# Column halves for the last rows, a masked table for the first unit, and a second queue for the tail stores

**Chip and metric.** One core of a Trainium2 chip. The time is device microseconds (us) of one execution. Runs of a kernel on one chip spread by up to 5 us.

## The reference

Sliding-window attention over q, k, v of shape (8, 8, 576, 64) makes x (8 batches, 576 tokens, 512 channels). Then comes a mix in the frequency domain:

```python
X = np.fft.rfft(x, axis=1)
Y[:, :64] = X[:, :64] times a complex 512 x 512 matrix per mode   # w_r, w_i: 134 MB read
y = np.fft.irfft(Y, n=S, axis=1)
u = x + y
out = u + np.maximum(u @ w_ch, 0.0)                                # 9.44 MB written
```

## The kernel before

For most of its time the kernel reads the 64 modes' weights. While they come, it collects the spectral rows Z (Y as rows of modes) and ZW (Y times w_ch) of the modes that are done. When the last weight has landed, the last mode's rows have to be scaled, transposed, multiplied by w_ch and patched into Z and ZW with small DMAs. Then 18 output units (128 tokens of two batches each; units 8 and 17 are the "tail" units of 64-token remainders) are made and stored.

The passage from the last weight to the first unit:

```python
yq, yT = heads[LAST]
nc.scalar.mul(yq[96:], acc[96:], 2.0 / S)
scatter([nc.sync, nc.scalar, nc.sync, nc.sync, nc.scalar, nc.gpsimd, nc.gpsimd, nc.gpsimd],
        yq, LAST, 6, 8, lambda b: Z[:, b])           # 8 small DMAs, two of them from ScalarE
... # 4 transposes into tr
nc.vector.tensor_copy(yT[:, :, 96:], tr[:, :, 96:])
... # heads["yw"] = late_channels(...): 4 matmuls with w_ch, then nc.scalar.copy(yw, zl)
take(1); begin(1); channels(1)
patch_channels([nc.sync] + [nc.gpsimd] * (B - 1), heads["yw"], LAST)
for step in ("a0 f0 a1 f1 a2 a3 f3 a5 f5 a10 f2 a8 f8 a12 f10 a9 f9 a11 f12 a14 f14 "
             "a16 f11 a17 f17 a4 f16 a6 f6 a7 a13 f4 f13 a15 f15 f7").split(): ...
```

A unit is made by `activate` (aN: matmuls into mm, relu by ScalarE into r; for the units in POOLED GpSimd adds the tokens to r) and `finish` (fN: matmuls into yy, for the others with the tokens added on TensorE; VectorE adds yy and r into o; o is stored). The first two units take the last rows of ZW not from the patched ZW but through a masked table FM, so they need not wait for the patches.

```python
POOLED, HALVES, FIRST = (2, 4, 7, 10, 11, 12, 16), (0, 1, 3, 5, 7), (0, 1)
...
for half in range(2):                                 # tail units: 64 partitions per store
    lo, hi = b + half + 2 * c.start, b + half + 2 * c.stop - 1
    nc.sync.dma_start(out=out[lo:hi:2, FULL * P :].rearrange("b p e -> p b e"),
                      in_=o[ROWS[half], c])
```

The softmax here doesn't subtract the row's maximum and nothing guards it: scores larger than these inputs give would overflow.

## Time and profile before

| | before |
|---|---|
| time, median of 3 runs (4 with the one beside the changed kernel's) | 450.82 us (450.8) |
| span of the profiled run | 449.1 us |
| last weight landed | 411.04 us |
| its last matmul ends | 412.26 us |
| first store issued | 417.79 us |
| last matmul ends | 440.5 us |
| last data of the stores | 447.5 us |

In a line of the chain of waits the columns are start, length and what held the end up. In a stretch of the window view come, after the stretch and its length, busy us (and instructions) of TensorE, its weight loads, VectorE, ScalarE and GpSimd, then TensorE's clock, the busy share of the 16 DMA engines, and GB/s. The prediction shows these lines for the kernel before.

### The profile page before, as it was taken

Reading aid. Unit: us, or ns where it says so; the run is one execution under the profiler, and the core shown is the slowest. Engines: PE = TensorE matmul, PEld = TensorE weight load, DVE = VectorE, ACT = ScalarE, POOL = GpSimd, SP = SyncE. Lnnn points to the kernel's source line nnn. Section 1 sums busy time; section 2 is a strip of 40 time slices with the busy share of each in tenths; the row PEclk is TensorE's granted clock in tenths of the full one; section 3 lists DMA queues with packets and bytes.
Section 4 is the critical chain, followed back from the end, with each engine's and each line's share of the span. In section 5 each row is a group of like instructions: output and inputs, shape, how many; then the busy total and the mean of one; then the engine's idle time right before and its main releaser. Section 6 shows DMA issues by size and latency. Waiting matters only on the chain.

```text
span 449.1 us, 7986 instructions
## 1 busy us (share of the span) xinstructions
PE 350.6 (78%) x3291; PEld 188.1 (42%) x3315; DVE 176.9 (39%) x321; ACT 152.2 (34%) x193; POOL 72.8 (16%) x124
## 2 busy tenths in 40 slices
PE   4688899999866485467477768999999998866992
PEld 3456777777654132122122334444444443322330
DVE  7879899998832011000010223121221203301783
ACT  6869899999810000000000011112211110100771
POOL 8600101012411100100000000000000000074771
PEclk8689999999999568875965799999999999999998
DMA  8999999999999999999999999999999999994698
GB/s 281 311 314 322 302 311 313 316 306 241 207 292 316 306 286 316 326 379 424 420 420 422 422 422 419 419 422 417 422 419 419 422 420 421 420 392 146 239 304 307
DMA packets 53607, 157.03 MB, mean 350 GB/s; under 512 B 5172, under 2 KB 24388, under 8 KB 41156
## 3 DMA queue, kind: packets, MB, share of 16 engines
q1 hardware_dynamic: 47708, 140.54, 81.4%
q0 software_dynamic: 5856, 15.99, 18.1%
q8 instruction: 26, 0.43, 0.4%
q14 instruction: 9, 0.07, 0.0%
q10 hardware_dynamic: 8, 0.00, 0.0%
HBM read 162.53 MB, written 9.44 MB: 383 GB/s over the span
## 4 chain that ended last, share of the span: by engine, by line
DMA 60%; PE 27%; DVE 8%; issue 2%; SPq 1%; POOL 0%; ACT 0%; DVEq 0%; POOLq 0%
DMA w<-in_moe_w_i_dram 19%; DMA w<-in_moe_w_r_dram 16%; DMA vr<-in_v_dram 15%; PE acc L822 10%; DMA vr<-in_moe_w_i_dram 7%; PE my L671 7%; DVE vb L233 3%; PE tr L650 2%; PE my L628 2%; DMA kr<-in_k_dram 2%; DMA out_dram<-o 1%; PE yy L762 1%; PE mm L704 1%; PE yy L748 1%; DVE vt L235 1%
## 5 line engine op out<-in xcount | busy, mean ns | idle before, releaser
L822 PE MATMUL acc<-w,XC 128*32 128x512 bf16 x456 | 127.9, 449 | 45.5 <-DMA w<-in_moe_w_r_dram 26.8
L822 PEld LDWEIGHTS <-XC 128*32 128x32 bf16 x508 | 59.4, 140 | 126.3 <-issue 89.5
L294 ACT ACTIVATE att<-sc 128x1024 bf16<-128x1024 f32 x64 | 64.1, 1032 | 7.7 <-PE sc L284 7.7
L605 ACT CAST ZW<-zw 128x512 bf16<-128x512 f32 x8 | 4.7, 585 | 161.4 <-DVE Z L607 126.3
L577 DVE TENSOR_SCALAR yq<-acc 128x512 bf16<-128x512 f32 x13 | 8.9, 688 | 100.2 <-PE acc L822 100.2
L680 ACT CAST XW<-my 128x512 bf16<-128x512 f32 x36 | 19.3, 589 | 75.4 <-PE my L628 75.4
L618 POOL DMA_DIRECT2D Z<-yq x19 | 9.7, 517 | 213.5 <-issue 207.9
L331 PE MATMUL av<-vb,att 128*128 128x132 bf16 (+1 forms) x576 | 38.4, 217 | 5.8 <-DVE x L347 4.1
L331 PEld LDWEIGHTS <-att 128*128 128x128 bf16 x704 | 36.5, 98 | 11.4 <-DVE x L347 8.4
L652 DVE COPY xT<-tr 128x1024 bf16<-128x1024 bf16 x18 | 12.5, 692 | 69.7 <-PE tr L650 69.7
L671 PE MATMUL my<-wch,xT 128*64 128x512 bf16 x288 | 34.5, 382 | 0.8 <-DVE xT L652 0.8
L256 ACT COPY qkT<-tp 128x1152 bf16<-128x1152 bf16 x30 | 33.4, 1115 | 3.0 <-PE tp L250 2.4
L284 PE MATMUL sc<-qkT 64*64 64x256 bf16 (+2 forms) x640 | 25.4, 266 | 5.2 <-ACT qkT L256 1.6
L347 DVE TENSOR_TENSOR x<-av,rec 128x640 bf16<-128x640 f32 x32 | 26.4, 825 | 1.1
L774 DVE TENSOR_TENSOR o<-yy,r 128x1024 f32<-128x1024 f32 (+1 forms) x23 | 21.7, 988 | 7.6 <-ACT r L739 5.9
L671 PEld LDWEIGHTS <-xT 128*64 128x64 bf16 x288 | 14.8, 109 | 18.9 <-issue 6.9
L284 PEld LDWEIGHTS <-qkT 64*64 64x64 bf16 x640 | 14.6, 109 | 19.1 <-issue 15.8
L233 DVE CAST vb<-vr 64x1024 bf16<-64x1024 f32 x32 | 22.2, 694 | 0.2
L607 DVE CAST Z<-z 64x512 bf16<-64x512 f32 x16 | 11.0, 689 | 24.6 <-PE z L600 24.4
L305 DVE TENSOR_TENSOR att<-att,mask 128x1024 bf16<-128x1024 bf16 x32 | 20.6, 683 | 0.0
L739 ACT ACTIVATE r<-mm 128x1024 f32<-128x1024 f32 (+1 forms) x23 | 18.4, 839 | 5.8 <-PE mm L628 4.9
L523 POOL COPY gate<-x 1x1 bf16<-1x1 bf16 x11 | 5.8, 525 | 85.8 <-DVE x L347 85.8
(119 smaller groups left out, 372.6 us busy)
## 6 DMA issues: line engine op xcount, KB each, us to landing
w<-in_moe_w_i_dram SPq DMA_DIRECT2D x52, 1024.0 KB, 18.0
w<-in_moe_w_r_dram SPq DMA_DIRECT2D x45, 1024.0 KB, 17.9
qr<-in_q_dram SPq DMA_DIRECT2D x16, 576.0 KB, 9.6
kr<-in_k_dram SPq DMA_DIRECT2D x16, 576.0 KB, 6.3
vr<-in_v_dram SPq DMA_DIRECT2D x64, 128.0 KB, 6.1
w<-in_moe_w_r_dram POOLq DMA_DIRECT2D x16, 512.0 KB, 17.2
out_dram<-o SPq DMA_DIRECT2D x11, 512.0 KB, 3.6
out_dram<-o SPq DMA_DIRECT2D x14, 256.0 KB, 3.7
```

The lines of the kernel that those rows point to most:

```text
L233: nc.vector.tensor_copy(self.vb[u % 2][row, :, :, :, W * half : W * half + D], src[row, :2])
L256: (self.nc.vector.tensor_copy if u < 2 and w == "q" else self.nc.scalar.copy)(dst.rearrange("q h (p j) -> q h p j", j=TPP), tp.rearrange(" ...
L284: nc.tensor.matmul(sc[64 * half : 64 * half + 64, e, j * 256 + c0 : j * 256 + c0 + n], lhsT=qkT[row, 1, h, k0 + j : k0 + P : 2], rhs=qkT[r ...
L294: self.nc.scalar.activation(self.att[u % 2][:, kt * 8 * P : (kt + 1) * 8 * P], sc.rearrange("p e n -> p (e n)"), AF.Exp, scale=1.0 / math. ...
L305: nc.vector.tensor_tensor(out=rows, in0=rows, in1=self.table[:, heads], op=ALU.mult)
L331: nc.tensor.matmul(bank[:, qt * W : qt * W + rhs[j].shape[1]], lhsT=att[:, o : o + P], rhs=rhs[j], start=(n == 0 and j == 0), stop=(n == l ...
L347: nc.vector.tensor_tensor(out=self.x[:, b, :, cs].rearrange("p t (h d) -> p h t d", h=2), in0=tiles[:, :, :, :D], in1=rec.unsqueeze(-1).br ...
L671: nc.tensor.matmul(mm[ROWS[half]], lhsT=lhsT, rhs=wch[:, dt], start=(dt == 0), stop=False, skip_group_check=True,)
L680: nc.scalar.copy(XW[:, j, n], mms[n])
L739: nc.scalar.activation(r[:, c], mm[:, c], AF.Relu)
L774: nc.vector.tensor_tensor(out=o[:, c], in0=yy[:, c], in1=r[:, c], op=ALU.add)
L822: nc.tensor.matmul(into[32 * (i // 2) : 32 * (i // 2) + 32], lhsT=window[a], rhs=w[a], start=(ri == 0 and a == 0), stop=(ri == (m > 0) and ...
```

## The change

The intent is to shorten the passage and to keep the stores fed and fast. The last rows go through ScalarE, transposes and w_ch in two halves of 256 columns, and ScalarE issues no DMA any more. Unit 0 takes its Y rows through FM as well (its other Y matmuls move in front of the last weight). The second half of each tail store goes to GpSimd's queue. The order of units, and which units GpSimd adds to, change too. One more thing is in the diff: a matmul into zl whose result is overwritten (L889, issued at 412.55, 0.39 us) stands before the transposes.

```diff
-        POOLED, HALVES, FIRST = (2, 4, 7, 10, 11, 12, 16), (0, 1, 3, 5, 7), (0, 1)
+        POOLED, HALVES, FIRST = (3, 4, 8, 12, 16), (0, 1, 2, 7, 15), (0, 1)
 ...
+            if j == 0:
+                last_rows(yys[0][0], 0, heads["yq"])
 ...
-                    nc.sync.dma_start(
+                    (nc.gpsimd if half else nc.sync).dma_start(
                         out=out[lo:hi:2, FULL * P :].rearrange("b p e -> p b e"),
 ...
                     add_tokens(0)
+                    finish_tokens(0)                 # in front of the last weight's matmuls
 ...
-        nc.scalar.mul(yq[96:], acc[96:], 2.0 / S)
-        scatter([nc.sync, nc.scalar, nc.sync, nc.sync, nc.scalar, nc.gpsimd, ...
+        for i, c in enumerate(sides):                # two halves of 256 columns
+            nc.scalar.mul(yq[96:, c], acc[96:, c], 2.0 / S)
+            ... # 2 transposes
+            nc.vector.tensor_copy(yT[:, 2 * i : 2 * i + 2, 96:], tr[:, 2 * i : 2 * i + 2, 96:])
+        patch([(nc.sync, 0), (nc.sync, 1)], yq, LAST, lambda b: Z[:, b])
+        patch([(nc.gpsimd, b) for b in (2, 3, 4)], yq, LAST, lambda b: Z[:, b], 6)
+        yw = F[:, : DM // (2 * NM)].rearrange("p a b -> p (a b)")   # a dead table as buffer
+        for i, c in enumerate(sides):
+            late_channels(zl[i], yT, yw, c)
 ...
+        channel_rows([(nc.sync, 0)] + [(nc.gpsimd, b) for b in (1, 2, 3)])
+        patch([(nc.gpsimd, b) for b in (5, 6, 7)], yq, LAST, lambda b: Z[:, b], 6)
+        channel_rows([(nc.gpsimd, b) for b in (4, 5, 6, 7)])
-        ... "a0 f0 a1 f1 a2 a3 f3 a5 f5 a10 f2 a8 f8 a12 f10 a9 f9 a11 f12 a14 f14 "
-            "a16 f11 a17 f17 a4 f16 a6 f6 a7 a13 f4 f13 a15 f15 f7"
+        ... "a0 f0 a1 f1 a3 a2 f2 a7 f7 a4 f3 a5 f5 a16 a9 f4 f9 a12 a17 f16 f17 a8 "
+            "a13 f12 f13 a11 f11 a14 f8 a10 f14 a6 f10 f6 a15 f15"
```

More of the change, by code (lines that the diff above doesn't have):

```diff
@@ L547, in late_end @@
             nc.vector.tensor_scalar_mul(yq[rows], acc[rows], 2.0 / S)
-            scatter([nc.gpsimd] * B, yq, g, 0, 2 * n, lambda b: Z[:, b])
+            patch([(nc.gpsimd, b) for b in range(2 if g == LAST else 0, B)],
+                  yq, g, lambda b: Z[:, b], 0, 2 * n)
             yield
@@ L560, in late_end, with late_channels @@
             zw = ps.tile([P, DM], FP32, tag="zw", bufs=1, name="zw")
-            patch_channels([nc.gpsimd] * B, late_channels(zw, yT), g)
-        def late_channels(zw, yT):
+            yw = pool.tile([P, DM], BF16, tag="yq", bufs=3)
+            late_channels(zw, yT, yw, slice(0, DM))
+            patch([(nc.gpsimd, b) for b in range(B)], yw, g, lambda b: ZW[:, b // 2, 1])
+        def late_channels(zw, yT, yw, c):
             for et in range(4):
-                nc.tensor.matmul(zw, lhsT=yT[:, et], rhs=wch[:, et],
+                nc.tensor.matmul(zw[:, c], lhsT=yT[:, et], rhs=wch[:, et, c],
                                  start=(et == 0), stop=(et == 3))
-            yw = pool.tile([P, DM], BF16, tag="yq", bufs=3)
-            nc.scalar.copy(yw, zw)
-            return yw
-        def patch_channels(queues, yw, g):
-            scatter(queues, yw, g, 0, 8, lambda b: ZW[:, b // 2, 1])
+            nc.scalar.copy(yw[:, c], zw[:, c])
         def quad_end(acc, g):
@@ L612, in stream_spectra, with patch @@
             spectra(hf, bp, z, zw)
-        def scatter(queues, rows, g, lo, hi, dst):
-            for b in range(B):
+        def patch(todo, rows, g, dst, lo=0, hi=8):
+            for queue, b in todo:
                 r = 64 * (b % 2) + 8 * (g % 8)
-                queues[b].dma_start(out=dst(b)[r + lo : r + hi],
-                                    in_=rows.rearrange("(k v) e -> k v e", v=16)[lo:hi, b])
+                queue.dma_start(out=dst(b)[r + lo : r + hi],
+                                in_=rows.rearrange("(k v) e -> k v e", v=16)[lo:hi, b])
         def tokens(st, half):
@@ L717, in channels, with last_rows @@
                         spread(mm[:, n], row, b + row + 2 * n, 1, st, 0)
-        def last_channels(j):
-            mm, st = mms[j][0], units[j][1]
+        def last_rows(ps, j, rows):
+            st = units[j][1]
             for n in range(2):
-                nc.tensor.matmul(mm[:, n], lhsT=FM[:, n, st * P : (st + 1) * P], rhs=heads["yw"],
+                nc.tensor.matmul(ps[:, n], lhsT=FM[:, n, st * P : (st + 1) * P], rhs=rows,
                                  start=False, stop=True, skip_group_check=True)
@@ L731, in activate @@
             if j in FIRST:
-                last_channels(j)
+                last_rows(mms[j][0], j, heads["yw"])
             else:
@@ L749, in add_tokens, with finish_tokens @@
                                  start=True, stop=False, skip_group_check=True)
-        def finish(j):
-            b, st = units[j]
-            if j not in yys:
-                take(j)
-            if j and j not in POOLED:
-                add_tokens(j)
-            (yy, slot), r = yys.pop(j), rs.pop(j)
-            o = heads["out"].tile([P, 2, DM], FP32, tag="o", bufs=5, name="o")
+        def finish_tokens(j):
+            yy, b, st = yys[j][0], *units[j]
             for n in range(2):
@@ L772, in finish @@
                     )
+        def finish(j):
+            b, st = units[j]
+            if j == 0:
+                last_rows(yys[0][0], 0, heads["yq"])
+            else:
+                if j not in yys:
+                    take(j)
+                if j not in POOLED:
+                    add_tokens(j)
+                finish_tokens(j)
+            (yy, slot), r = yys.pop(j), rs.pop(j)
+            o = heads["out"].tile([P, 2, DM], FP32, tag="o", bufs=5, name="o")
             for c in parts(j):
@@ L878 @@
         yq, yT = heads[LAST]
-        nc.scalar.mul(yq[96:], acc[96:], 2.0 / S)
-        scatter([nc.sync, nc.scalar, nc.sync, nc.sync, nc.scalar, nc.gpsimd, nc.gpsimd, nc.gpsimd],
-                yq, LAST, 6, 8, lambda b: Z[:, b])
-        tr = lps.tile([P, 4, P], BF16, tag="tr", name="tr")
-        for et in range(4):
-            nc.tensor.transpose(tr[:, et, 96:], yq[96:, et * P : (et + 1) * P], ident[96:, 96:])
-        nc.vector.tensor_copy(yT[:, :, 96:], tr[:, :, 96:])
-        with ExitStack() as zctx:
-            zps = zctx.enter_context(tc.tile_pool(name="zps", bufs=1, space=PSUM))
-            heads["yw"] = late_channels(zps.tile([P, DM], FP32, name="zl"), yT)
+        zctx = ExitStack()
+        zps = zctx.enter_context(tc.tile_pool(name="zps", bufs=1, space=PSUM))
+        zl = [zps.tile([P, DM], FP32, name=f"zl{i}") for i in range(2)]
+        nc.tensor.matmul(zl[1], lhsT=ident, rhs=wch[:, 0], start=True, stop=True)
+        sides = (slice(0, DM // 2), slice(DM // 2, DM))
+        tr = lps.tile([P, 4, P], BF16, tag="tr", name="tr")
+        for i, c in enumerate(sides):
+            nc.scalar.mul(yq[96:, c], acc[96:, c], 2.0 / S)
+            for et in (2 * i, 2 * i + 1):
+                nc.tensor.transpose(tr[:, et, 96:], yq[96:, et * P : (et + 1) * P],
+                                    ident[96:, 96:])
+            nc.vector.tensor_copy(yT[:, 2 * i : 2 * i + 2, 96:], tr[:, 2 * i : 2 * i + 2, 96:])
[4 more added lines that the diff above has]
+            late_channels(zl[i], yT, yw, c)
+        zctx.close()
         lctx.close()
@@ L891 @@
             tc.tile_pool(name="tps", bufs=1, side="right", space=PSUM, reuse_waits="tile"))
+        heads.update(yq=yq, yw=yw)
         heads["mm"].append(last)
@@ L898 @@
         channels(1)
-        patch_channels([nc.sync] + [nc.gpsimd] * (B - 1), heads["yw"], LAST)
-        for step in ("a0 f0 a1 f1 a2 a3 f3 a5 f5 a10 f2 a8 f8 a12 f10 a9 f9 a11 f12 a14 f14 "
-                     "a16 f11 a17 f17 a4 f16 a6 f6 a7 a13 f4 f13 a15 f15 f7").split():
+        channel_rows = partial(patch, rows=yw, g=LAST, dst=lambda b: ZW[:, b // 2, 1])
+        channel_rows([(nc.sync, 0)] + [(nc.gpsimd, b) for b in (1, 2, 3)])
+        patch([(nc.gpsimd, b) for b in (5, 6, 7)], yq, LAST, lambda b: Z[:, b], 6)
+        channel_rows([(nc.gpsimd, b) for b in (4, 5, 6, 7)])
+        for step in ("a0 f0 a1 f1 a3 a2 f2 a7 f7 a4 f3 a5 f5 a16 a9 f4 f9 a12 a17 f16 f17 a8 "
+                     "a13 f12 f13 a11 f11 a14 f8 a10 f14 a6 f10 f6 a15 f15").split():
             {"a": activate, "f": finish}[step[0]](int(step[1:]))
```

## The prediction

> **What bounds the kernel now.** I read the page first, then the chain of waits from 380 us on, then the timeline from 405 us on, and last the engines and the DMA in stretches of that tail. Up to about 409 us the weight stream sets the pace (its DMA lines hold 19%, 16% and 7% of the page's chain), and the change leaves that part as it is. All that matters lies in the last 40 us.
>
> The chain of waits (start us, us, what):
>
> ```profile
> 408.77 1.07 PE acc L822 x4
> ...
> 411.14 1.14 PE acc L822 x4
> 412.27 0.02 issue
> 412.29 0.60 ACT yq L879
> 412.89 0.28 issue
> 413.17 0.49 POOL Z L618
> 413.66 1.51 DMA Z<-yq
> 415.18 0.59 ACT yw L568
> 415.76 0.04 issue
> 415.81 0.59 PE mm L723 x2
> ...
> 434.60 0.61 SPq L784
> 435.21 0.05 issue
> 435.26 4.85 DMA out_dram<-o
> ```
>
> The last weight is multiplied until 412.27. Then a serial passage of 3.54 us leads to the first matmul that makes an output (415.81). From there the chain is TensorE without a break until 433.27, and after that the stores. So the tail has three stages: the passage, a stage at TensorE's pace, and a drain of the stores.
>
> The timeline of the passage:
>
> ```profile
> 412.91 1.85 ACTq L618 DMA_DIRECT2D Z<-yq  x2
> 413.52 1.04 PE L565 MATMUL zl<-wch,xT 128*128 128x512 bf16 x4 [0.32 <-DVE xT L885]
> 415.17 0.58 ACT L568 CAST yw<-zl 128x512 bf16<-128x512 f32 x1 [2.29 <-DMA Z<-yq]
> 417.79 6.83 SPq L776 DMA_DIRECT2D out_dram<-o  x9
> ```
>
> zl is complete at 414.56, but ScalarE copies it only at 415.17: its own two DMA issues last until 414.76, and the profile names a Z DMA as what the copy waited for (its buffer comes from the pool that those DMAs read). That is 0.6 us of avoidable wait. The first store is issued at 417.79, 5.52 us after the last weight.
>
> Stretches of the store stage (the last two numbers of a line are DMA share and GB/s):
>
> ```profile
> 418.00:426.00 8.00, 7.85 (x70) 2.43 (x74) 6.32 (x9) 6.19 (x10) 6.03 (x6) 1.00 0.85 306
> 426.00:427.00 1.00, 0.95 (x10) 0.32 (x8) 1.00 (x2) 0.93 (x2) 0.45 (x1) 1.00 0.58 219
> 427.00:429.00 2.00, 2.00 (x20) 0.40 (x18) 1.70 (x3) 1.50 (x2) 1.68 (x1) 1.00 0.72 143
> 429.00:436.00 7.00, 6.85 (x57) 2.05 (x58) 5.69 (x5) 5.21 (x6) 5.30 (x3) 1.00 1.03 367
> 436.00:439.00 3.00, 3.00 (x31) 0.99 (x24) 2.74 (x3) 2.08 (x4) 2.40 (x2) 1.00 0.94 274
> 439.00:447.00 8.00, 1.43 (x6) 0.39 (x4) 3.36 (x4) 0.94 (x1) 0.83 (x1) 0.85 1.03 383
> ```
>
> The page counts 9.44 MB written. At 383 GB/s that is 24.6 us, yet the data move from about 418.6 to 447.5, that is 28.9 us: 4.3 us of store time are lost. Each stretch loses length x (383 - rate) / 383: 1.6 us in the first (part of it before any store), 0.4 in 426 to 427, 1.25 in 427 to 429, 0.3, and 0.85 in 436 to 439. The 1.25 and the 0.85 follow the two pairs of tail-token stores (issued from 426.19 and 434.60). One microsecond shows how:
>
> ```profile
> 428.00:429.00 1.00, 1.00 (x14) 0.20 (x10) 1.00 (x2) 0.93 (x1) 0.68 (x1) 1.00 0.98 182
> ...
> 433.00:434.00 1.00, 1.00 (x13) 0.26 (x10) 0.65 (x1) 0.37 (x2) 0.92 (x1) 1.00 1.04 391
> ```
>
> At 428 the DMA engines are as busy as at 433 and move less than half. This is slow data, not missing data.
>
> **What the Trainium skill says.** (1) "SBUF — State Buffer", section "Door 1: The DMA port swizzle": partitions 0 to 63 reach only 8 of the 16 ports, 64 to 127 the other 8. A tail store reads 64 partitions; 182 against 391 GB/s agrees. (2) Same page, "Can I just issue two DMAs to hit both halves?": it answers no, with 6% gained. That speaks against one part of the change; nothing in the trace before tests it. (3) "DMA: Bandwidth & Descriptors", "Queues, rings and completion order": each DMA engine takes turns, packet by packet, between the queues that have work. So a half on a second queue at least interleaves with the other half or with the next full store. Not tested before either. (4) "TensorE: Matmul & The Clock Gate", "Back-to-back issue gap": a 512-column matmul every 216 ns, 256 columns about 109. The chain's pairs of 0.43 us (0.215 each) agree.
>
> **The change part by part.** (a) Unit 0's two Y matmuls move in front of the last weight. The last weight DMA is issued at 391.5 and lands after 19.6 us, at 411.1; the matmuls for it start at 411.14, directly behind other work of TensorE, so the two extra ones delay them: 2 x 0.215 = +0.43 us on the path. Their counterparts with the masked table take, after the passage, the place of the two removed: no change there.
>
> (b) The passage. Before, from 412.27 to 415.81: 0.62 scaling, 0.35 to the copy of the transposes, 0.28 to zl, 1.04 zl, 0.61 wait, 0.64 copy and start. After: two scalings of 256 columns end together about where one of 512 did (0.64); transposes and copy of the second half about 0.45 (before 0.58, for half the size); zl in two halves, 4 x 0.107 + 0.19 until ScalarE may copy the first, 0.43 later the second; that last copy is half as long (0.33); no DMA issues on ScalarE and a dead table as the buffer, so no wait. Sum: 0.64 + 0.45 + 0.62 + 0.43 + 0.33 + 0.08 = 2.55. But unit 1's begin and channel matmuls (0.64) stand behind zl on TensorE and end near 2.6, so I take 2.65: -0.89 us. With (a) the first store comes 0.46 us earlier, near 417.33.
>
> (c) Units added on GpSimd go from 7 to 5. Each unit that goes back to TensorE adds two identity matmuls, by the timeline 1.52 us between begins against 1.10, so 2 x 0.42, less the tail unit that goes the other way (same 0.5 in another place): TensorE's sum over units 2 to 17 goes from 22.5 to 23.3 us, and TensorE ends at 440.9 instead of 440.5. GpSimd has 13 patch issues (about 0.53 each) after the passage instead of 10, so its first addition can start near 420.8 instead of 419.84. The new order places that unit's finish third, where VectorE wants it at about 422.9: just in time.
>
> (d) The tail halves go to two queues. If they then use both port groups, the loss of 1.25 + 0.85 us shrinks to the gaps for missing data; I count 1.2 us of 2.1 regained.
>
> (e) The order of units. Dealing out 1.2 us per VectorE output and 1.37 us per full store (524 KB at 383 GB/s) from 417.3 on, stores wait for data about 1.5 us in all before 426 and hardly after. Before, the first two stretches lose 2.0 us, and part of 427 to 429 is missing data too (share 0.45 in its first half, by the same view). I count 0.8 us regained.
>
> Sum: -0.46 - 1.2 - 0.8 = -2.5 us; 450.82 - 2.5 = 448.3. Cross-check: TensorE ends at 440.9, VectorE needs two halves of 0.62 to 0.68 after it, issue and start about 0.9, data 0.7, and from the last data (447.5) to the end of the span 1.6 pass: 445.6 at the very least, 3.5 under 449.1. So time can hardly go below 447, since TensorE is the next bound.
>
> **The rivals.** Rival 1: the two queues do not help (the skill's 6%). Then the tail stores still need 2 x 64-partition time, gains are (b), (e) and little else: about 449.5. For it: the page's statement. Against it: the packets of the second queue can interleave with a full store. Rival 2: TensorE's or GpSimd's extra work becomes the bound. 13 patches hold GpSimd longer; a patch that lands late (one took 3.5 us once stores ran, 419.24 to 422.73) can stop TensorE at unit 16, which needs the last batches early. One such stop costs 0.5 to 1.5 us: 449 to 450. Rival 3: all is hidden, because the stores at the end are limited by bytes alone. Against it: 4.3 us of 28.9 are lost, so bytes alone do not set the end. It would give 450.4 (only the earlier start counts). Rival 4: more works out than I count (all 2.1 us of the tails and no stalls): 447.0.
>
> **Range and chances.** Predicted 448.3 us; 8 times in 10 between 446.8 and 450.0: the low end is TensorE's bound with some error in (c), the high end is rival 1 or 2 with noise (the three runs before differ by 1 us). A change of 2% is 9 us, more than twice all lost store time, so faster by over 2% has 1%; slower by over 2% would take 9 us of stalls, which nothing in the trace suggests: 1%. Within 2%: 98%.
>
> **What would show it.** Right: last weight's matmuls ending near 412.7; ScalarE's copies in halves with no wait for a DMA; first store near 417.3; full rate (over 330 GB/s) in the microseconds after the tail stores; TensorE's last matmul near 441 and last data near 445. Wrong: the last weight not delayed (then (a) is mis-sized); a stretch with share near 1.0 and about 180 GB/s after the tail stores (rival 1); TensorE or VectorE idle for GpSimd or a patch DMA (rival 2). A different landing time of the last weight would shift everything.

## The result and the profile after

The changed kernel takes 452.56 us (451.44 to 453.07, 4 runs) against 450.8 us before: slower by 0.32%, with a 95% interval of 0.10% to 0.55%. A ratio here is the mean time of one kernel's runs over that of the other's of the same rounds, so it is not quite the ratio of the medians. I had predicted 448.3 with a range up to 450.0: wrong.

The passage did what it should. The chain of waits of the changed kernel, its passage and its end:

```profile
411.57 1.06 PE acc L829 x4
412.63 0.02 issue
412.65 0.39 ACT yq L893
413.04 0.05 issue
413.08 0.22 PE tr L895 x2
...
413.77 1.11 PE zl L568 x8
414.89 0.34 PE mm L702 x4
415.23 0.22 PE mm L626 x4
415.45 0.54 PE mm L721 x2
...
441.20 0.69 DVE o L780
```

From 412.63 to 415.45 it lasts 2.82 us (3.54 before), and no ScalarE wait for a DMA is in it. VectorE's last output, too, ends at 441.89, no later than before. What is lost comes after that, in the drain. The timeline of the changed kernel at the first tail pair and at GpSimd's first additions:

```profile
417.37 13.30 SPq L782 DMA_DIRECT2D out_dram<-o  x13
...
421.38 4.23 POOL L740 TENSOR_TENSOR r<-r,x 128x1024 f32<-128x1024 f32 x2
...
423.56 4.75 DVE L780 TENSOR_TENSOR o<-yy,r 128x1024 f32<-128x1024 f32 x4 [0.90 <-POOL r L740]
...
431.43 0.73 SPq L790 DMA_DIRECT2D out_dram<-o  x1
...
431.70 0.66 POOL L790 DMA_DIRECT2D out_dram<-o  x1 [0.86 <-DVE o L780]
```

The first store is issued at 417.37, 0.42 us earlier than before. GpSimd's first addition starts at 421.38, and VectorE waits 0.90 us for it. Stretches of one microsecond of the changed kernel, at the first tail pair and at the end:

```profile
433.00:434.00 1.00, 1.00 (x12) 0.31 (x4) 1.00 (x2) 0.64 (x1) 1.00 (x1) 1.00 1.00 184
434.00:435.00 1.00, 1.00 (x12) 0.28 (x12) 0.92 (x2) 0.50 (x2) 0.52 (x1) 1.00 1.08 285
435.00:436.00 1.00, 1.00 (x13) 0.26 (x10) 1.00 (x2) 0.92 (x2) 0.00 (x0) 1.00 0.88 272
...
446.00:447.00 1.00, 0.00 (x0) 0.00 (x0) 0.00 (x0) 0.00 (x0) 0.00 (x0) 0.50 0.88 336
447.00:448.00 1.00, 0.00 (x0) 0.00 (x0) 0.00 (x0) 0.00 (x0) 0.00 (x0) 0.50 0.35 135
448.00:449.00 1.00, 0.00 (x0) 0.00 (x0) 0.00 (x0) 0.00 (x0) 0.00 (x0) 0.50 0.08 29
```

The same end of the kernel before:

```profile
446.00:447.00 1.00, 0.00 (x0) 0.00 (x0) 0.00 (x0) 0.00 (x0) 0.00 (x0) 0.50 1.04 391
447.00:448.00 1.00, 0.00 (x0) 0.00 (x0) 0.00 (x0) 0.00 (x0) 0.00 (x0) 0.50 0.27 100
```

Two things are to be seen. The first half of the tail pair still runs at about half rate (184 GB/s at share 1.00), and by the packet records it runs alone: GpSimd's half, issued at 431.70, has its first packet at 434.20, 2.5 us later. And before, all DMA engines work until about 447.2 and stop together, while in the changed kernel the share falls from 0.88 over 0.35 to 0.08: a few engines work on alone for over a microsecond. By the packet records what they still move are SyncE's stores, not GpSimd's, at 84 ns a packet, as in the full stores before: these engines are not slow at the end, they have more left to do. The last data come at 448.7 instead of 447.5, although the last store is issued only 0.3 us later (444.18 against 443.85).

### The profile page after: what moved, and what is told of

It reads as the page before. It is cut to its first block, busy times and chain, and to the rows that moved or that the text cites. A ratio compares the mean times of both kernels' runs of the same rounds, so it can differ in the third digit from the quotient of the medians.

```text
span 450.1 us, 8002 instructions
## 1 busy us (share of the span) xinstructions
PE 355.8 (79%) x3301; PEld 191.5 (43%) x3326; DVE 176.9 (39%) x322; ACT 152.7 (34%) x195; POOL 70.5 (16%) x125
## 4 chain that ended last, share of the span: by engine, by line
DMA 47%; PE 34%; DVE 12%; issue 2%; ACT 1%; POOL 1%; SPq 0%; DVEq 0%; POOLq 0%; ACTq 0%
DMA w<-in_moe_w_r_dram 25%; PE acc L829 10%; DMA w<-in_moe_w_i_dram 10%; PE my L669 7%; DMA vr<-in_moe_w_r_dram 7%; DMA vr<-in_v_dram 5%; DVE vb L233 3%; PE tr L648 2%; PE my L626 2%; PE av L331 2%; DVE x L347 2%; PE yy L754 1%; PE mm L702 1%; DVE att L305 1%; PE yy L746 1%
## 5 line engine op out<-in xcount | busy, mean ns | idle before, releaser
L829 PE MATMUL acc<-w,XC 128*32 128x512 bf16 x456 | 129.4, 450 | 45.3 <-DMA w<-in_moe_w_r_dram 25.8
L284 PE MATMUL sc<-qkT 64*64 64x256 bf16 (+2 forms) x640 | 25.7, 269 | 4.8 <-ACT qkT L256 1.2
```

Of the source, the lines that this page charges most:

```text
L284: nc.tensor.matmul(sc[64 * half : 64 * half + 64, e, j * 256 + c0 : j * 256 + c0 + n], lhsT=qkT[row, 1, h, k0 + j : k0 + P : 2], rhs=qkT[r ...
L829: nc.tensor.matmul(into[32 * (i // 2) : 32 * (i // 2) + 32], lhsT=window[a], rhs=w[a], start=(ri == 0 and a == 0), stop=(ri == (m > 0) and ...
```

## The experiments

**How they are compared.** Up to the last weight's landing the kernels do the same, but that landing fell anywhere between 410.5 and 413.9 us in the profiled runs, and this noise is larger than the differences sought. So beside the time ratio I use the stretch from the last weight's landing (from the DMA completions in the trace) to the end of the span. Two control runs say how well it repeats: unaltered copies of both kernels gave 38.04 us (38.06 at first) and 39.06 us (39.05). "Engines full until" is when 14 or more packets were last in flight, counted in the trace's packet records (good to about 0.2 us). A stretch is called dry when the DMA engines have too few stores to move, and a trickle when only a few of them still move data. All times but the ratio are us after the landing.

| kernel | time against before (95%) | first store | engines full until | last data | end |
|---|---|---|---|---|---|
| before; again | 0.998 (0.995 to 1.001) | 6.74; 6.62 | 36.2; 36.1 | 36.46; 36.45 | 38.06; 38.04 |
| changed; again | 1.0032; 1.0031 (1.000 to 1.006) | 6.30; 6.12 | 35.5; 36.0 | 37.61; 37.63 | 39.05; 39.06 |
| e1 tail on one queue | 0.9977 (0.995 to 1.0005) | 6.30 | 35.9 | 36.19 | 37.51 |
| e2 before + two queues | 0.9994 (0.997 to 1.002) | 6.63 | 35.8 | 36.94 | 38.19 |
| e3 passage only | 1.0044 (1.002 to 1.007) | 6.39 | 38.1 | 38.38 | 39.69 |
| e4 order only | 0.9987 (0.996 to 1.001) | 6.71 | 35.6 | 36.36 | 37.97 |
| e5 tail: SyncE and ScalarE | 1.0011 (0.997 to 1.005) | 6.09 | 35.4 | 36.74 | 38.04 |
| e6 unit 5 before 3 | 1.0011 (0.998 to 1.004) | 6.29 | 35.6 | 36.58 | 37.89 |
| e8 tail: both GpSimd | 1.0028 (0.999 to 1.007) | 6.34 | 36.3 | 38.46 | 40.01 |
| e9 tail early | 1.0008 (0.997 to 1.0045) | 6.33 | 35.7 | 36.94 | 38.25 |
| e10 tail early, two queues | 1.0001 (0.997 to 1.003) | 6.18 | 35.6 | 37.21 | 38.62 |
| e12 unit 3 on TensorE | 0.9977 (0.995 to 1.0005) | 6.39 | 35.4 | 36.42 | 37.72 |
| e13 full store on GpSimd | 0.9967 (0.994 to 0.999) | 6.28 | 35.3 | 37.48 | 38.83 |

**The changed kernel and the kernel before, again.** No edit.

> The changed kernel once more, unaltered, as a control beside the other runs: 0.3% above before, and from the landing of the last weight to the end of the span 39.0 us again (the kernel before has 38.06), with DMA engines finishing at different times. If that stretch comes out under 38.5, one profile is not enough to compare tails by.

> The kernel before, unaltered, as a control of the method: ratio 1.000 within 0.2%, and from the landing of the last weight to the end of the span 38.06 us again, within 0.2 us. If the stretch differs by more than 0.5 us, differences of tails of that size mean nothing.

Measured: stretches of 39.06 and 38.04 us, ratios 1.0031 and 0.998. So the stretch repeats to 0.02 us for these two, and the change costs 1.0 us of it. Of the other 0.4 of the 1.4 us (0.31% of 452), 0.25 us is outside the span: in the changed kernel's runs the time exceeds the span by 2.2 us on average, in those of before by 1.97. I have no explanation for these 0.25 us; e3, without a GpSimd store, shows 2.3. What is left, 0.15 us, is well within the interval.

**e1, the tail stores on one queue**

```diff
-                    (nc.gpsimd if half else nc.sync).dma_start(
+                    nc.sync.dma_start(
```

> The changed kernel with both halves of the tail stores back on the SyncE queue. Theory A (the half on the GpSimd queue starts about 1.7 us after its issue, so the halves don't run together, and it leaves the DMA engines unevenly loaded at the end: in the changed kernel the last data trickle from 447 to 448.7 us): about 450.0 us, 2.4 us below the changed kernel, and the last data stop at once on all engines. Theory B (the new order and the later GpSimd additions cost the time; the stores ran dry from 424.5 to 425.5 us): within 0.5 us of the changed kernel's 452.5.

The stretch is 37.51: 1.54 us shorter than the changed kernel's from this edit alone, and 0.54 shorter than before. The end of e1 by the window view:

```profile
448.00:449.00 1.00, 0.00 (x0) 0.00 (x0) 0.00 (x0) 0.00 (x0) 0.00 (x0) 0.50 0.94 361
449.00:450.00 1.00, 0.00 (x0) 0.00 (x0) 0.00 (x0) 0.00 (x0) 0.00 (x0) 0.50 0.18 68
```

A sharp end again (this run's last weight landed 2.1 us later, so its clock times are later). The time, 451.7 us, was 1.0 us under before, with an interval that just reaches 1; it ends at 1.0005, where the changed kernel's begin, at 1.0010 and 1.0002 (runs of other rounds). Theory A (the second queue) is borne out in the stretch, against theory B (order). How it costs can be read from the semaphore that tells of a store's landing, which counts 16 arrivals: of the last store's, the ninth comes 36.35 us after the landing of the last weight in e1 and 36.51 in the changed kernel, the last one 36.52 and 37.95. So most of the last store is done at nearly the same time, and a few parts of it are late. In the changed kernel first and last arrival lie at most 0.2 us apart in the five stores before the first tail pair, 2.7 us in SyncE's half of the second pair and still 2.2 us in the last store (in e1 1.7 and 1.0). The absolute time that I had expected, 450.0, was not reached.

**e2, two queues alone, on the kernel before**

```diff
-                    nc.sync.dma_start(
+                    (nc.gpsimd if half else nc.sync).dma_start(
```

> The kernel before with only the second half of each tail store moved to the GpSimd queue. Theory A: slower than before by 1 to 2.5 us (451.8 to 453.3), with a stretch where the two halves do not overlap and a trickle at the end. Theory B: as before, 450.8, or up to 1.5 us faster if the halves share the ports as I predicted.

The stretch is only 0.13 to 0.15 us longer, and the time is the same: what theory B said for the time, and not the 1 to 2.5 us of theory A. But in the packet records the engines' ends spread again: full until 35.8, last data at 36.94, while in the kernel before all stop within 0.3 us. Here the second pair is issued earlier (23.5 us after the landing, 25.7 in the changed kernel), so more of the drain is still to come.

**e3, the passage and the masked table alone**: e1 with the order, POOLED and HALVES of before.

> The changed kernel with the order of units, the units on GpSimd, the halved units and the tail stores of before: only the passage in column halves and unit 0 by the masked table remain. First store about 0.4 us earlier than before under every theory. Theory A: 450.2 to 450.8, the gain of the start partly lost in the drain. Theory B: the same, 450.3. Theory C (the three extra patch issues on GpSimd alone cost the time): 451.5 or more.

The earlier start is there (6.39), yet the stretch is 1.6 us longer and the time 0.44% worse: theory C. TensorE's waits in e3:

```profile
PE mm L626 <- DMA ZW<-F: 1.3, 1, 1.3
```

TensorE stops 1.3 us for a ZW patch, since GpSimd now issues 13 patches instead of 10 and the old order asks for the last batches early; its last matmul ends 31.07 us after the landing (29.45 before). So the new order is needed to make the new passage pay; neither can be judged alone.

**e4, the order alone, on the kernel before**: only `POOLED, HALVES` and the list of steps.

> The kernel before with only the order of units, the units on GpSimd and the halved units of the change. Theory A: 450 to 451. Theory B: 452 or more, with the stores dry near 425 us because VectorE waits for a GpSimd addition.

37.97, a gain of 0.1 us (theory A), where I had predicted 0.8. By the packet records the dry stretch near the first tail pair is gone (before 203, 109, 178, 279 and 334 KB in the five us from 15 us after the landing; now 369 or more in all five, at the price of one dry us, 98 KB, earlier), but the tail pair's slow stretch, which before lay partly in that dry time, now stands in full behind a backlog (221, 178, 285, 338 from 21 us on). Against 383 KB in a microsecond, both kernels fall short in these stretches by what 2.1 us would move. The loss moved.

**e5, the second half on ScalarE's queue**

```diff
-                    (nc.gpsimd if half else nc.sync).dma_start(
+                    (nc.scalar if half else nc.sync).dma_start(
```

> The changed kernel with the second half of a tail store on ScalarE's queue instead of GpSimd's. Theory A1 (what costs is GpSimd's queue, with its late start and its uneven hand-out to the DMA engines): the two halves run side by side at over 300 GB/s, no trickle, end 37.0 us after the last weight, about 1.5% of the tail under the one-queue version (37.5). Theory A2 (any second queue leaves the engines uneven, or two halves can't share the ports, as the skill's page says): 38 us or more after the last weight. ScalarE may lose up to 1 us to waiting for VectorE before its issue; seen as an idle stretch of ScalarE.

38.04: better than GpSimd's queue by 1.0, worse than one queue by 0.5. The timeline and the window view of e5 show that two queues don't help, at the first pair and, in the last line, at the second:

```profile
433.04 0.73 SPq L790 DMA_DIRECT2D out_dram<-o  x1
433.04 0.73 ACTq L790 DMA_DIRECT2D out_dram<-o  x1
```

```profile
434.00:435.00 1.00, 0.19 (x5) 0.15 (x8) 0.82 (x1) 1.00 (x2) 0.02 (x1) 1.00 0.84 217
435.00:436.00 1.00, 1.00 (x11) 0.35 (x11) 0.15 (x1) 1.00 (x2) 1.00 (x1) 1.00 0.95 197
436.00:437.00 1.00, 1.00 (x11) 0.20 (x9) 1.00 (x2) 0.73 (x1) 1.00 (x1) 1.00 1.02 283
...
442.00:443.00 1.00, 0.81 (x11) 0.38 (x4) 1.00 (x2) 0.69 (x3) 0.00 (x0) 1.00 0.94 272
```

The halves of the first pair are issued in the same instant, but by the packet records SyncE's moves from 434.41 to 435.9, its packets of 2 KB at about 160 ns (84 ns in full stores), and ScalarE's first packet starts at 435.78. These halves go one after the other. Those of the second pair do overlap (ScalarE's packets run from 440.68 to 443.41, SyncE's half, by the order of its queue, from about 441.9 to 443.2), and no more is moved for it: 272 GB/s at share 0.94, and 260 at 0.98 in the changed kernel's second pair (440 to 441), where e1 with one queue has 244 and 279 (442 to 444). So theory A2 holds for the missing gain, and A1 for the greater part of the drain's loss. ScalarE's in-order wait for VectorE also showed: it stood idle 2.73 us at the first pair.

**e6, unit 5 before unit 3**: in e1's list `a7 f7 a5 f5 a4 f3` for `a7 f7 a4 f3 a5 f5`.

> One queue for the tail stores, and units 5 and 3 exchanged in the order (a5 f5 a4 f3 for a4 f3 a5 f5), so that VectorE has unit 5 to do while GpSimd still adds to unit 3. If the dry stretch of the stores near 424.5 to 425.5 us costs what it lasts, the end comes 0.6 to 0.9 us earlier than in the one-queue version: 36.7 us after the last weight, 0.4% under before. If the stores are bound by bytes later anyway, nothing: 37.5.

No gain, 37.89 (e1 has 37.51): the dry stretch only moved, from 281 and 147 KB at 13 and 14 us after the landing to 295 and 104 KB at 16 and 17.

**e8, both halves on GpSimd's queue**

> The changed kernel with both halves of the tail stores on GpSimd's queue: one queue, but the software one. Theory A1 (GpSimd's queue itself): slow like the changed kernel or slower, 39 us after the last weight, with a trickle at the end. Theory A2 (two queues that compete): the trickle is gone or small, since neither pair is split, though the pair still competes with SyncE's next stores: 38 us.

The worst, 40.01, with a trickle from 36.3 to 38.5. So the pair need not be split; on GpSimd's queue, apart from the other stores, it costs even more when whole.

**e13, one full store on GpSimd's queue**: e1 with

```diff
-                    nc.sync.dma_start(
+                    (nc.gpsimd if j == 14 else nc.sync).dma_start(
```

for the 128-partition stores.

> The one-queue version of the change, with one full 128-partition store near the end (unit 14) on GpSimd's queue and both tail halves on SyncE's. If any store on a second queue leaves the DMA engines uneven in the drain: a spread of 1 us or more between the first engines out of work and the last, end 38.3 us or later after the last weight (one-queue version 37.5). If only the 64-partition halves on a second queue do it: sharp end, 37.4 to 37.7.

38.83, 1.3 us longer than e1, and the trickle is back. Its end by the window view:

```profile
446.00:447.00 1.00, 0.00 (x0) 0.00 (x0) 0.00 (x0) 0.00 (x0) 0.00 (x0) 0.50 0.60 229
447.00:448.00 1.00, 0.00 (x0) 0.00 (x0) 0.00 (x0) 0.00 (x0) 0.00 (x0) 0.50 0.12 47
448.00:449.00 1.00, 0.00 (x0) 0.00 (x0) 0.00 (x0) 0.00 (x0) 0.00 (x0) 0.50 0.03 12
```

So a full store on GpSimd's queue does it too, not only a half; on ScalarE's queue no full store was tried. (Its time ratio, 0.9967 in 4 runs, points the other way, so that e13 rests on one profile; it also shows how little a ratio of this size says when the landing of the last weight moves by 3 us.)

**e9, e10, e12, meant to beat both kernels.** e9: e1 with `a8 f8` moved behind `f2` and unit 8 out of POOLED. e10: the same with two queues. e12: e1 with unit 3 out of POOLED.

> Meant to beat both: the passage of the change, one queue for the tail stores, and the first tail unit moved up to fifth place and off GpSimd, where the store stage still waits for data, so that its slow half-stores lie in time that is lost anyway and VectorE has work while GpSimd adds to unit 3. If slow tail stores cost only where the DMA has a backlog: one of the two slow stretches (1.3 us) is mostly hidden, the dry stretch near 13 us after the last weight goes: end 36.5 to 37.0 us after the last weight, against 37.5 with the order of the change and 38.1 before; the time 0.4% under before. If the loss only moves: 37.5.

> The same with the second half of a tail store on GpSimd's queue. If the second queue's harm comes from the drain (engines left uneven by the last tail pair), it stays: 1.0 to 1.5 us slower than the one-queue version of this order. If it came from the place of the first tail pair, the two are equal within 0.3 us.

> Meant to beat both: the one-queue version with unit 3 added on TensorE instead of GpSimd, so that VectorE does not wait 0.9 us for it while the stores run dry. If that wait is worth its length: 36.8 to 37.2 us after the last weight against 37.5, and 0.3% under before. If TensorE's extra 0.43 us in the ramp, or the next GpSimd addition, takes it back: 37.5.

e9 lost 0.7 us to e1 (38.25): the stores ran drier, not fuller, early on (100, 104 and 188 KB in three successive us). e10 is 0.4 us longer than e9, less than the 1.0 to 1.5 expected if the drain alone did the harm, and more than the 0.3 for the other theory: between the two. e12 removed VectorE's wait for GpSimd and the dry stretch (311 and 381 KB where e1 has 281 and 147), yet ended 0.2 us later than e1; its engines were full until 35.4 instead of 35.9, but spread by 1 us at the end. So an uneven drain also comes with one queue, and the wait that e12 removed was not what ate the gain. None of the three beats e1. e1 is the best kernel by its stretch (37.51, one profile), and its time is not clear of noise.

## Why the prediction was wrong

By its own steps:

- (a) The last weight delayed by two matmuls: predicted +0.43, measured about +0.3 (its matmuls end 1.54 and 1.37 us after the landing, before 1.22 and 1.10). Right, if a little smaller.
- (b) The passage: predicted -0.89, measured -0.72 (2.82 us for 3.54), again a little smaller. The net start, -0.46 predicted, came out at -0.42 on the clock and -0.47 after the landing. Right. The 0.215 us for a matmul behind (a) and (c) is what the trace shows. The prediction names 216 ns from the Trainium skill, "TensorE: Matmul & The Clock Gate", "Back-to-back issue gap"; that section gives it for a matmul by itself and about 131 ns for a stream, which the chain's pairs of 0.43 us don't show.
- (c) TensorE's end: predicted 0.4 us later, measured 0.3 later (after the landing). Right. GpSimd's first addition was put at 420.8 and VectorE's need at 422.9, "just in time"; it started at 421.38 and VectorE waited 0.90 us. A miss of 0.6 us, but e12 shows that taking the wait away brings no earlier end.
- (d) is the step that failed: "I count 1.2 us of 2.1 regained" by two queues. Measured (changed kernel against e1): 1.54 us lost. Two things were wrong in it. The two halves move no faster from two queues: in the first pair they go one after the other, even when issued together (e5), and in the second they overlap at 260 to 272 GB/s, so the slow stretch stays. And the second queue leaves the DMA engines with unequal ends, which I had not thought of at all: between the last time that all worked and the last data lie 0.3 us in the kernel before, in e1 and in e3, and 1.1 to 2.2 us in every kernel with a store on a second queue (e2, e5, e8, e10, e13 and the changed kernel). One queue alone does not rule it out: e4, e6, e9 and e12 have 0.8 to 1.2. Rival 1 had the first half of this, named from the skill's page, and I set it aside on an argument of interleaving; even its 449.5 left out the drain.
- (e) The order: predicted 0.8 us regained, measured 0.1 alone (e4). I counted the waiting for data and the slow tail stores as separate losses. In the kernel before they overlapped in part, so filling the first laid bare the second. A term of the sum that was mis-sized by counting twice.
- The cross-check, by which only TensorE stood in the way of an earlier end, looked at when work is issued, and not at when the last DMA engine is done.

With the measured terms: start -0.47, order with the new passage -0.07 (e1's 37.51 against 38.05, less the start), two queues +1.54, together +1.0, which is the measured 39.05 less 38.05. It closes by construction, for the parts are not independent: two queues alone cost 0.13 on the kernel before (e2), and the passage alone made it 1.6 us longer (e3).

**What stays open.** Why a second queue leaves the engines uneven is not shown, nor why some one-queue orders do so by less. The packet records do not name the engine; at the very end nearly always two packets are in flight in e8 (37 to 38 us after the landing) and in e13 (36.2 to 36.8), so by this estimate about two engines are the last; whether they are always the same two stays open. So does why the second queue's half waits in the first pair. Why e2 lost only 0.1 us with the same unevenness is explained by its earlier second pair in argument only. A tail layout that stores all 128 partitions at once, which might remove the half-rate stretches, was not tried; it needs another arrangement of the tail's rows on TensorE.

## What to carry to other kernels

When stores drain at full DMA rate at the end of a kernel, keep them on one queue unless a run says otherwise: here a second one did not join two 64-partition halves into one full-rate store, and it made the last DMA engines finish later than the others (0.1 to 2.5 us on the stretch, by the order of units and the queue). Count a slow transfer and a wait for data in the same stretch once, since filling the wait exposes the transfer. And when a noisy common part precedes the change, compare the stretch behind it (here from the last weight's landing), after checking with unaltered copies how well it repeats.

## What the Trainium skill lacked or had wrong

- "DMA: Bandwidth & Descriptors", "Issuing engines are not separate DMA queues" says that several issuing engines only save issue time. The runs add that they can cost: one full store of 18 units' on GpSimd's queue ended the kernel 1.3 us later (38.83 against 37.51 after the last weight), both tail halves there 2.5 us later (40.01). The section gives no such cost.
- Same page, "Queues, rings and completion order" says that each engine takes turns between queues packet by packet. In e5 two stores issued on two queues at 433.04 hardly overlapped: the second's first packet started at 435.78, when the first's last were moving. The second pair of the same run did overlap (from about 441.9 to 443.2), so the runs bear the turns out in one case and not in the other.
